# One SBUF residue for all moving tiles of a token group, and sixteen residues in turn

## The chip, the cores and the metric

The kernel runs on one core of one Trainium2 chip. The metric is the device time of one execution in microseconds (us), measured on the core. Three executions of the kernel before took 3115.2, 3115.26 and 3116.17 us; the median is 3115.26 us. Each engine runs its own instruction stream: PE multiplies matrices, and its weight loads (PEld) are shown apart from its matmuls; DVE and ACT do elementwise work, POOL as well; SP issues most of the DMAs.

## The reference

A long convolution is followed by a two-layer network. Cut to what matters:

```python
def _attn_ref(x, v, pos_emb, w1, w2):            # x, v: 4 x 12480 x 128
    h = np.maximum(pos_emb @ w1, 0.0) @ w2 * np.exp(-0.01 * pos)[:, None]
    y = np.fft.irfft(np.fft.rfft(x * v, n=2 * S, axis=1) * np.fft.rfft(h, n=2 * S, axis=0)[None], n=2 * S, axis=1)[:, :S]
    return x * y

def _moe_ref(x, w_in, w_out):                    # x: 49920 x 128; w_in: 128 x 2048; w_out: 2048 x 128
    h = np.maximum(x @ w_in, 0.0)
    return h * h @ w_out
```

## The kernel before

The convolution is a transform written as matmuls in four stages (s1 to s4), for the filter and for each of the four batches. The second part, the two-layer network, takes the 49,952 columns of s4's output in 98 token groups: two of 446 columns, then 512 or 510 columns each. The inner dimension of 2048 goes in eight blocks f of 256 columns. The network's stream of work is written out in one loop over groups and blocks; the transform stages of the next batch are generators from which the loop takes a step at three places (adv). The last groups, after all transform work, are called the tail here; the profile shows it from about 2670 us on.

Every float32 operand of the network is split in a high and a low part in a rounded float32 format, and one product is three matmuls (mm3, lines 92 to 97): high weights by high data (L95), low weights by high data (L96), high weights by low data (L97). For each group and block there are twelve of them: six that multiply w_in by the group's tokens (moving tiles zh and zl, into the PSUM tile A), and six that multiply w_out by the squared activations of an earlier block (moving tiles gh and gl, into O, or into F in the tail). The weights are the stationary operand, and each of these matmuls loads its own 128 by 128 weights first; the loads of the next matmul run beside the current one. In all there are 98 x 8 x 12 = 9408 such matmuls of the 13,442 that the program has.

Between them ACT makes r = relu(A) (L799) and squares (L802, L806), and DVE makes the rest (L804, L813) and gl = square - gh (L818). m_g and m_l do this; zsplit makes zh and zl of the next group (L781, L782) after zload has fetched it (zi).

Where the tiles lie. All are float32, two buffers each. The address of a tile within a partition is counted in bytes, and its residue here is that address modulo 512. As the program was built, the weight tiles wt start at 196,576 and follow each other 2048 bytes apart, with slices 512 bytes apart, so every weight slice of the network has residue 480. The tiles zh, zl, gh, gl and r of pool mp are 2048 or 4096 bytes long and stacked below the weights, so they have residue 480 too: zh at 159,712 and 161,760, gh at 176,096 and 180,192, gl at 184,288 and 188,384. In the tail a second pool, tp, on the other side of SBUF holds r, gh and gl of the odd blocks (line 882, `tail[0] if tail and f % 2 else mp`), and there gh and gl have residue 128 (gh at 131,712 and 135,808). In s4 the moving tiles ah and al have residue 128 or 448, and their weights, the four slices of a tile tb 448 bytes apart, many residues.

Of the kernel before, what the change touches and what calls it, by code (L numbers as in the profile page):

```python
# [7 lines left out]
F32 = mybir.dt.float32  # L8
F32R = mybir.dt.float32r
# [7 lines left out]
D = 128  # L17
# [9 lines left out]
GT = NT // NG  # L27
NS = NF // 2
GM = 512
NM = 2 + (B * NT - 2 * GT + GM - 1) // GM  # L30
GE = (B * NT - 2 * GT) // (NM - 2) // 2 * 2
GN = [GT, GT] + [GE + 2 * (k < (B * NT - 2 * GT - GE * (NM - 2)) // 2) for k in range(NM - 2)]
# [6 lines left out]
TH = 4  # L39
CW = 256  # L40
NCW = DFF // CW


@with_exitstack
def hyena_moe_kernel(
# [34 lines left out]
    def pool(name, side="left", **kw):  # L80
        return tc.tile_pool(name=name, bufs=kw.pop("bufs", 2), side=side, reuse_waits="tile", **kw)
# [17 lines left out]
    def load_weights(wp):  # L99
        raws = []  # L100
        for c in range(2 * NCW):
            raw = wp.tile([128, CW, 2], I32, tag="w", name="raw", bufs=2 * NCW)
            src = (w_in if c < NCW else w_out).bitcast(I32)[:, c % NCW * 2 * CW : (c % NCW + 1) * 2 * CW]
            nc.sync.dma_start(out=raw.rearrange("p a b -> p (a b)"), in_=src)
# [3 lines left out]
    def convert_weights(p, wp, raws, wt, chunks):  # L108
        V = nc.vector
        for c in chunks:  # L110
            low, high = raws[c][:, :, 0], raws[c][:, :, 1]
            mag, top, sgn = (p.tile([128, CW], I32, tag=k, name="cv") for k in ("cm", "ct", "cs"))
            mf = mag.bitcast(F32)
            tf = top.bitcast(F32)
            V.tensor_scalar(out=top, in0=high, scalar1=0x7FFFFFFF, scalar2=None, op0=ALU.bitwise_and)
            yield
            V.tensor_scalar(out=mf, in0=tf, scalar1=2.0**-15, scalar2=122880.0, op0=ALU.max, op1=ALU.min)
            yield
            V.tensor_scalar(out=top, in0=mag, scalar1=3, scalar2=0x7FFFFFFF, op0=ALU.logical_shift_left, op1=ALU.bitwise_and)
            yield  # L120
            V.tensor_scalar(out=mag, in0=low, scalar1=1, scalar2=None, op0=ALU.logical_shift_right)
            nc.gpsimd.tensor_copy(mf, mag)
            yield
            V.tensor_scalar(out=sgn, in0=high, scalar1=-0x80000000, scalar2=0x40000000, op0=ALU.bitwise_and, op1=ALU.bitwise_xor)
            yield
            V.tensor_tensor(out=top, in0=top, in1=sgn, op=ALU.bitwise_xor)
            wt[c] = wp.tile([128, 2, CW], F32R, tag="w", name="wt", bufs=2 * NCW)
            hi12, lo12 = wt[c][:, 0, :], wt[c][:, 1, :]
            nc.gpsimd.tensor_copy(hi12, tf)
            yield  # L130
            V.tensor_scalar(out=sgn, in0=top, scalar1=-0x800000, scalar2=None, op0=ALU.bitwise_and)
            yield
            V.scalar_tensor_tensor(out=mf, in0=mf, scalar=2.0**-51, in1=sgn.bitcast(F32), op0=ALU.mult, op1=ALU.mult)
            yield
            V.tensor_sub(out=tf, in0=tf, in1=hi12.bitcast(F32))
            yield
            V.tensor_add(out=lo12, in0=tf, in1=mf)
            yield
# [546 lines left out]
    def run(gen):  # L685
        for _ in gen:
            pass
# [6 lines left out]
    def take(name, *args, **kw):  # L694
        held[name] = ExitStack()
        return held[name].enter_context(pool(name, *args, **kw))
# [47 lines left out]
    cvp = take("cvp")  # L744
    conv = [convert_weights(cvp, wp, raws, wt, range(k, 2 * NCW, 2)) for k in range(2)]
    run(stage2(True, True, "left", during_s2f))
# [5 lines left out]
    held["tbb"].close()  # L752

    mp = ctx.enter_context(pool("mp", "right"))
    head = [mp.tile([D, GM], F32R, tag=k, name=k)[:, :GT] for k in ("zh", "zl")]
    s4 = stage4(0, done, take("t1p"))
    run(stage3(True, ft[0], lambda t: t == -12 and step(s4)))
    idle(12)
# [1 line left out]
    def wi(k, h, f):  # L760
        return wt[k * NCW + f // 2][:, h, f % 2 * 128 : (f % 2 + 1) * 128]

# [11 lines left out]
            at += n  # L774
        return zi

    def zsplit(zi):
        n = zi.shape[1]
        hi = mp.tile([D, GM], F32R, tag="zh", name="zh")[:, :n]
        lo = mp.tile([D, GM], F32R, tag="zl", name="zl")[:, :n]  # L780
        nc.scalar.copy(hi, zi)  # L781
        nc.gpsimd.tensor_sub(out=lo, in0=zi, in1=hi.bitcast(F32))  # L782
        return hi, lo

    def m_h(zT, f):
        A = psa.tile([128, 2, 512], F32, tag="A", name="A")
        for t in range(2):
            mm3(A[:, t, : zT[0].shape[1]], (wi(0, 0, 2 * f + t), wi(0, 1, 2 * f + t)), zT)
        return A

    def m_g(A, p, n, between, way):

        r = p.tile([128, 2, GM], F32, tag="r", name="r")[:, :, :n]
        hi = p.tile([128, 2, GM], F32R, tag="gh", name="gh")[:, :, :n]
        h = A[:, :, :n]
        nc.scalar.activation(r, h, AF.Relu)  # L799
        between()  # L800
        if way != "b":
            nc.scalar.activation(hi, r, AF.Square)  # L802
        if way == "p":
            nc.vector.scalar_tensor_tensor(out=h, in0=h, scalar=0.0, in1=r, op0=ALU.max, op1=ALU.mult)  # L804
            return p, h, hi, way
        nc.scalar.activation(r, r, AF.Square)  # L806
        return p, r, hi, way

    def m_l(st, share):
        p, g, hi, way = st  # L810
        lo = p.tile([128, 2, GM], F32R, tag="gl", name="gl")[:, :, : g.shape[2]]
        if way == "b":
            nc.vector.tensor_copy(hi, g)  # L813
        if share:
            nc.gpsimd.tensor_sub(out=lo[:, 1, :], in0=g[:, 1, :], in1=hi[:, 1, :].bitcast(F32))
            nc.vector.tensor_sub(out=lo[:, 0, :], in0=g[:, 0, :], in1=hi[:, 0, :].bitcast(F32))
        else:
            nc.vector.tensor_sub(out=lo, in0=g, in1=hi.bitcast(F32))  # L818
        return hi, lo
# [3 lines left out]
    def m_o(i, f, hl):  # L823
        if f == 0:
            O[0] = bank() if tail and not nxt[0] else pso.tile([128, 512], F32, tag="O", name="O")
        o = O[0][:, : GN[i]]
        for t in range(2):
            mm3(o, (wi(1, 0, 2 * f + t), wi(1, 1, 2 * f + t)), (hl[0][:, t, :], hl[1][:, t, :]), first=(f == 0 and t == 0), last=(f == NS - 1 and t == 1))
        if f == NS - 1:
            return i, o  # L830
        return None

    def m_out(last):
        if last is not None:
            i, o = last
            ot = mp.tile([D, GM], F32, tag="ot", name="ot", bufs=1)[:, : GN[i]]
            nc.scalar.copy(ot, o)
            nc.sync.dma_start(out=out[:, GO[i] : GO[i] + GN[i]], in_=ot)
# [11 lines left out]
    def adv(k):  # L850
        if k is None or nxt[0] == k:
            nxt[0] = next(stream, 0)

    def ready(i):
        b, at = divmod(GO[i] + GN[i] - 1, NT)
        while done[b] < 2 * (at // GT + 1):
            adv(None)

    def way(n):
        if not nxt[0]:  # L860
            return "b"
        if stage[0] == "s2":
            return "t" if n % 3 else "p"
        return "b" if stage[0] == "s3" else "p"

    late, pend, tail = [], [], []
# [4 lines left out]
    for i in range(NM):  # L871
        for f in range(NS):
            adv(1)
            A = m_h(zT, f)
            last = m_o(*pend.pop(0)) if len(pend) > 1 else None
            adv(2)
            if not nxt[0] and not tail:
                tail.append(ctx.enter_context(pool("tp")))
            late.append((i, f, m_g(A, tail[0] if tail and f % 2 else mp, GN[i], lambda: m_out(last), way(i * NS + f))))
            while len(late) > len(tail):  # L880
                x, y, st = late.pop(0)
                pend.append((x, y, m_l(st, False)))
            if i + 1 < NM:
                if f == (1 if i else 3):
                    ready(i + 1)
                    zi = zload(i + 1)
                if f == (4 if i else 6):
                    nzT = zsplit(zi)
            adv(3)
            n = i * NS + f  # L890
            if stage[0] != since[0]:
                since = stage[0], n + 4
            owed += EXTRA[done[1] > 0]
            if owed >= 1 and stage[0] in (("s3", "s4") if done[1] else ("s2", "s3", "s4")) and nxt[0] == 1 and n >= since[1]:
                owed -= 1
                since = stage[0], n + 3
                for k in range(1, 4):
                    adv(k)
        if i + 1 < NM:
            zT = nzT  # L900
    for x, y, st in late:
        pend.append((x, y, m_l(st, True)))
# [114 lines left out]
```

## Time and profile before

| what | value |
|---|---|
| median of three executions | 3115.26 us |
| span of the profiled execution, first to last instruction | 3112.0 us |
| what lies around the span, by the median | 3.3 us |
| PE busy | 3072.7 us, 99% of the span |
| PEld busy | 2579.8 us, 83% |
| DVE, ACT, POOL busy | 82%, 78%, 48% |
| granted TensorE clock, mean | 0.999 of full speed |

The time of the profiled execution itself is shown as its span alone, so the time of a run is taken as the span and 3.3 us. A matmul's row gives its whole passage through the engine, and matmuls overlap each other: one of 510 columns lasts about 390 ns, while the next starts about 228 ns after it. How fast the engine really goes is read from the starts in the timeline, or from a count of matmuls in a stretch of time.

### The profile page before, as it was taken

Reading aid. Unit: us, or ns where it says so; the run is one execution under the profiler, and the core shown is the slowest. Engines: PE = TensorE matmul, PEld = TensorE weight load, DVE = VectorE, ACT = ScalarE, POOL = GpSimd, SP = SyncE. Lnnn points to the kernel's source line nnn. Section 1 sums busy time; section 2 is a strip of 40 time slices with the busy share of each in tenths; the row PEclk is TensorE's granted clock in tenths of the full one; section 3 lists DMA queues with packets and bytes.
Section 4 is the critical chain, followed back from the end, with each engine's and each line's share of the span. In section 5 each row is a group of like instructions: output and inputs, shape, how many; then the busy total and the mean of one; then the engine's idle time right before and its main releaser. Section 6 shows DMA issues by size and latency. Waiting matters only on the chain.

```text
span 3112.0 us, 49107 instructions
## 1 busy us (share of the span) xinstructions
PE 3072.7 (99%) x16086; PEld 2579.8 (83%) x16086; DVE 2538.0 (82%) x3080; ACT 2419.1 (78%) x3130; POOL 1501.6 (48%) x1631
## 2 busy tenths in 40 slices
PE   9989999999999999999999999999999999999999
PEld 7767888888888888888888888888888888888887
DVE  7888898878877988878877898878877799777776
ACT  5556777777788777788888877787788887878787
POOL 1249765556544565546644575646644466000000
PEclk9999999999999999999999999999999999999999
DMA  5783574434200664434300375434410176100000
GB/s 184 263 294 99 137 166 137 124 111 145 67 21 15 151 161 132 130 91 127 115 15 21 80 176 144 133 92 121 124 51 14 36 168 156 33 24 24 24 26 20
DMA packets 342623, 323.11 MB, mean 104 GB/s; under 512 B 161968, under 2 KB 288800, under 8 KB 342368
## 3 DMA queue, kind: packets, MB, share of 16 engines
q1 hardware_dynamic: 313216, 272.25, 30.2%
q0 software_dynamic: 29152, 47.72, 6.4%
q8 instruction: 128, 2.10, 0.3%
q14 instruction: 127, 1.04, 0.1%
HBM read 231.78 MB, written 65.60 MB: 96 GB/s over the span
## 4 chain that ended last, share of the span: by engine, by line
PE 92%; POOL 2%; DMA 2%; DVE 2%; issue 1%; ACT 1%; SPq 0%; DVEq 0%; ACTq 0%; POOLq 0%
PE A L95 11%; PE A L97 11%; PE A L96 11%; PE O L97 9%; PE O L96 9%; PE O L95 9%; PE F L380 6%; PE F L492 6%; PE F L293 5%; PE F L97 4%; PE F L95 4%; PE F L96 4%; PE A L290 2%; PE A L291 1%; POOL W L405 1%
## 5 line engine op out<-in xcount | busy, mean ns | idle before, releaser
L799 ACT ACTIVATE r<-A 128x1024 f32<-128x1024 f32 (+2 forms) x784 | 803.8, 1025 | 420.8 <-PE A L97 407.0
L818 DVE TENSOR_TENSOR gl<-r,gh 128x1020 fp32r<-128x1020 f32 (+1 forms) x433 | 642.5, 1484 | 113.9 <-ACT r L806 80.0
L95 PE MATMUL A<-zh,wt 128*128 128x512 f32 (+2 forms) x1568 | 671.4, 428 | 0.9 <-DVE gl L818 0.9
L97 PE MATMUL A<-zl,wt 128*128 128x512 f32 (+2 forms) x1568 | 613.8, 391 | 0.0
L96 PE MATMUL A<-zh,wt 128*128 128x512 f32 (+2 forms) x1568 | 612.9, 391 | 0.0
L802 ACT ACTIVATE gh<-r 128x1024 fp32r<-128x1024 f32 (+2 forms) x461 | 486.9, 1056 | 62.8 <-PE O L96 57.2
L97 PE MATMUL O<-gl,wt 128*128 128x512 f32 (+2 forms) x1248 | 487.4, 391 | 4.2 <-DVE gl L818 4.2
L96 PE MATMUL O<-gh,wt 128*128 128x512 f32 (+2 forms) x1248 | 485.0, 389 | 0.0
L95 PE MATMUL O<-gh,wt 128*128 128x512 f32 (+2 forms) x1248 | 484.9, 389 | 0.0
L804 DVE SCALAR_TENSOR_TENSOR A<-A,r 128x1024 f32<-128x1024 f32 (+2 forms) x350 | 425.4, 1215 | 68.1 <-ACT r L799 66.5
L818 DVE TENSOR_TENSOR gl<-A,gh 128x1024 fp32r<-128x1024 f32 (+2 forms) x350 | 426.1, 1218 | 63.1 <-ACT gh L802 20.4
L806 ACT ACTIVATE r<-r 128x1020 f32<-128x1020 f32 (+1 forms) x434 | 460.3, 1061 | 12.5
L813 DVE CAST gh<-r 128x1020 fp32r<-128x1020 f32 (+1 forms) x323 | 225.6, 698 | 221.2 <-ACT r L806 152.7
L782 POOL TENSOR_TENSOR zl<-zi,zh 128x512 fp32r<-128x512 f32 (+2 forms) x97 | 126.4, 1303 | 522.4 <-ACT zh L781 506.1
L567 POOL TENSOR_TENSOR al<-W,ah 112x512 fp32r<-112x512 f32 x214 | 281.9, 1318 | 189.2 <-ACT ah L561 185.0
L501 POOL TENSOR_TENSOR W<-c 112x224 f32<-112x224 f32 x256 | 217.6, 861 | 285.7 <-ACT c L499 275.0
L97 PEld LDWEIGHTS A<-zl,wt 128*128 128x128 f32 x1568 | 294.6, 188 | 64.7
L95 PEld LDWEIGHTS A<-zh,wt 128*128 128x128 f32 x1568 | 295.5, 188 | 51.4 <-DVE gl L818 3.1
L96 PEld LDWEIGHTS A<-zh,wt 128*128 128x128 f32 x1568 | 296.2, 189 | 45.1
L417 POOL TENSOR_TENSOR W<-W,m 112x256 f32<-112x256 f32 x168 | 177.8, 1058 | 247.3 <-DVE m L415 233.1
L97 PEld LDWEIGHTS O<-gl,wt 128*128 128x128 f32 x1248 | 234.2, 188 | 54.5 <-DVE gl L818 5.9
L96 PEld LDWEIGHTS O<-gh,wt 128*128 128x128 f32 x1248 | 234.2, 188 | 50.6
(127 smaller groups left out, 5495.3 us busy)
## 6 DMA issues: line engine op xcount, KB each, us to landing
ht<-Hd SPq DMA_DIRECT2D x224, 256.0 KB
tb<-t POOLq DMA_DIRECT2D x224, 196.0 KB, 3.1
xt<-x SPq DMA_DIRECT2D x224, 112.0 KB
xt<-xs SPq DMA_DIRECT2D x96, 224.0 KB
vt<-vs SPq DMA_DIRECT2D x96, 224.0 KB
tb<-t2s SPq DMA_DIRECT2D x168, 112.0 KB
Hd<-he SPq DMA_DIRECT2D x28, 512.0 KB
zd<-zs SPq DMA_DIRECT2D x222, 64.0 KB
```

The source lines that it names most:

```text
L95: nc.tensor.matmul(o, lh, rh, start=first, stop=False)
L96: nc.tensor.matmul(o, ll, rh, start=False, stop=False)
L97: nc.tensor.matmul(o, lh, rl, start=False, stop=last)
L380: nc.tensor.matmul(U[:I, k * 256 : (k + 1) * 256], tb[:KP, k, :], a[:, k], start=True, stop=True)
L501: nc.gpsimd.tensor_sub(out=dst[:, 1], in0=c[:, :, 0:3:2], in1=c[:, :, 3:0:-2])
L567: eng.tensor_sub(out=lo, in0=w, in1=hi.bitcast(F32))
L799: nc.scalar.activation(r, h, AF.Relu)
L802: nc.scalar.activation(hi, r, AF.Square)
L804: nc.vector.scalar_tensor_tensor(out=h, in0=h, scalar=0.0, in1=r, op0=ALU.max, op1=ALU.mult)
L806: nc.scalar.activation(r, r, AF.Square)
L813: nc.vector.tensor_copy(hi, g)
L818: nc.vector.tensor_sub(out=lo, in0=g, in1=hi.bitcast(F32))
```

## The change

A helper `word` takes the place of the plain tile calls for zh, zl, gh and gl (SP = 128 floats, 512 bytes, more per tile): group i uses the tile from byte 32 * (i % 16) on. So all moving tiles of a group lie at one residue, 480 for group 0, 0 for group 1, 32 for group 2, and so on; after sixteen groups the row begins again, so the 98 groups go through it six times and two groups more. A tile of 88 floats in pool tp puts gh and gl of the tail's odd blocks at the same residue as those of its even blocks. The weights stay at residue 480, and r stays where its pool puts it, at residue 480 in mp.

```diff
+SP = 128
+TP = 88
...
-    head = [mp.tile([D, GM], F32R, tag=k, name=k)[:, :GT] for k in ("zh", "zl")]
+
+    def word(p, tag, i, n, t=None):
+        s = 8 * (i % 16)
+        w = p.tile([128, (t or 1) * GM + SP], F32R, tag=tag, name=tag)[:, s : s + (t or 1) * GM]
+        return w[:, :n] if t is None else w.rearrange("p (t n) -> p t n", t=t)[:, :, :n]
+
+    head = [word(mp, k, 0, GT) for k in ("zh", "zl")]
...
-    def zsplit(zi):
-        n = zi.shape[1]
-        hi = mp.tile([D, GM], F32R, tag="zh", name="zh")[:, :n]
-        lo = mp.tile([D, GM], F32R, tag="zl", name="zl")[:, :n]
+    def zsplit(i, zi):
+        hi, lo = (word(mp, k, i, GN[i]) for k in ("zh", "zl"))
...
-        hi = p.tile([128, 2, GM], F32R, tag="gh", name="gh")[:, :, :n]
+        hi = word(p, "gh", i, n, 2)
...
-        lo = p.tile([128, 2, GM], F32R, tag="gl", name="gl")[:, :, : g.shape[2]]
+        lo = word(p, "gl", i, GN[i], 2)
...
                 tail.append(ctx.enter_context(pool("tp")))
+                tail[0].tile([128, TP], F32, tag="tp", name="tp", bufs=1)
```

On every engine the instructions are the same, of the same shapes and in the same order. What differs in the built program is the start addresses of the four tiles (and those of r, which moves by whole multiples of 512 bytes in mp), and five instructions that wait for other semaphores, since the pools are some kilobytes larger and come to lie on other tiles that were there before: three on ACT at the start of the network, one more at the start of the tail that takes over its successor's wait, and the first L818 of the tail that writes in tp, on DVE, which now also waits for stores of s4 (L628).

## Rows read from the trace of the kernel before

**Rows 1.** The page, busy time: us, share of the span, instructions.
```profile
PE 3072.7 (99%) x16086; PEld 2579.8 (83%) x16086; DVE 2538.0 (82%) x3080; ACT 2419.1 (78%) x3130; POOL 1501.6 (48%) x1631
```
**Rows 2.** The page, chain that ended last, by engine.
```profile
PE 92%; POOL 2%; DMA 2%; DVE 2%; issue 1%; ACT 1%; SPq 0%; DVEq 0%; ACTq 0%; POOLq 0%
```
**Rows 3.** PE groups, shapes apart: count, busy us, mean ns, idle before.
```profile
L95 PE MATMUL A<-zh,wt 128*128 128x512 f32 x800 | 351.3, 439 | 0.8 <-DVE gl L818 0.8
L97 PE MATMUL A<-zl,wt 128*128 128x512 f32 x800 | 315.5, 394 | 0.0
L96 PE MATMUL A<-zh,wt 128*128 128x512 f32 x800 | 313.9, 392 | 0.0
L97 PE MATMUL O<-gl,wt 128*128 128x512 f32 x800 | 313.4, 392 | 4.2 <-DVE gl L818 4.2
L96 PE MATMUL O<-gh,wt 128*128 128x512 f32 x800 | 311.9, 390 | 0.0
L95 PE MATMUL O<-gh,wt 128*128 128x512 f32 x800 | 311.7, 390 | 0.0
...
L96 PE MATMUL A<-zh,wt 128*128 128x510 f32 x736 | 287.4, 390 | 0.0
L97 PE MATMUL A<-zl,wt 128*128 128x510 f32 x736 | 286.7, 390 | 0.0
...
L97 PE MATMUL O<-gl,wt 128*128 128x510 f32 x416 | 162.3, 390 | 0.0
L96 PE MATMUL O<-gh,wt 128*128 128x510 f32 x416 | 161.5, 388 | 0.0
L95 PE MATMUL O<-gh,wt 128*128 128x510 f32 x416 | 161.5, 388 | 0.0
...
L96 PE MATMUL F<-gh,wt 128*128 128x510 f32 x320 | 125.5, 392 | 0.0
L97 PE MATMUL F<-gl,wt 128*128 128x510 f32 x320 | 125.4, 392 | 0.0
...
L95 PE MATMUL F<-gh,wt 128*128 128x510 f32 x320 | 125.1, 391 | 0.0
```
**Rows 4.** PE timeline in the tail: start us, duration us, instruction.
```profile
3013.23 0.39 PE L95 MATMUL F<-gh,wt 128*128 128x510 f32 x1
...
3014.59 0.39 PE L95 MATMUL A<-zh,wt 128*128 128x510 f32 x1
...
3015.95 0.40 PE L95 MATMUL F<-gh,wt 128*128 128x510 f32 x1
...
3017.35 0.39 PE L95 MATMUL A<-zh,wt 128*128 128x510 f32 x1
```
**Rows 5.** Source L96: duration ns min/median/max, first and last start.
```profile
L96 PE MATMUL F<-ah,tb x448: 276/279/285, 329.3 to 2647.8; 112*112 112x256 f32 x150
...
L96 PE MATMUL F<-gh,wt x320: 387/395/397, 2672.9 to 3106.2; 128*128 128x510 f32 x160
```
**Rows 6.** Source L95 and L97, the same columns.
```profile
L95 PE MATMUL F<-ah,tb x448: 274/281/374, 329.1 to 2647.7; 112*112 112x256 f32 x150
...
L97 PE MATMUL F<-gl,wt x320: 387/394/398, 2673.1 to 3106.4; 128*128 128x510 f32 x160
```
**Rows 7.** PE timeline before the tail, the network's chain after a transform step.
```profile
995.97 0.48 PE L95 MATMUL A<-zh,wt 128*128 128x512 f32 x1
996.28 0.39 PE L96 MATMUL A<-zh,wt 128*128 128x512 f32 x1
...
997.44 0.39 PE L95 MATMUL O<-gh,wt 128*128 128x512 f32 x1
```
**Rows 8.** The page, costliest groups: DVE's and ACT's idle time, what ended it.
```profile
L799 ACT ACTIVATE r<-A 128x1024 f32<-128x1024 f32 (+2 forms) x784 | 803.8, 1025 | 420.8 <-PE A L97 407.0
L818 DVE TENSOR_TENSOR gl<-r,gh 128x1020 fp32r<-128x1020 f32 (+1 forms) x433 | 642.5, 1484 | 113.9 <-ACT r L806 80.0
```
**Rows 9.** Source L628, the stores of s4: duration, first and last start.
```profile
L628 SPq DMA_DIRECT2D zd<-zs x444: 407/556/1869, 339.1 to 2653.3; - x148
```

More of the change, by code (lines that the diff above doesn't have):

```diff
@@ L789, in m_h, with m_g @@
         return A
-    def m_g(A, p, n, between, way):
+    def m_g(A, p, i, between, way):
+        n = GN[i]
         r = p.tile([128, 2, GM], F32, tag="r", name="r")[:, :, :n]
-        hi = p.tile([128, 2, GM], F32R, tag="gh", name="gh")[:, :, :n]
+        hi = word(p, "gh", i, n, 2)
         h = A[:, :, :n]
@@ L804, in m_g @@
             nc.vector.scalar_tensor_tensor(out=h, in0=h, scalar=0.0, in1=r, op0=ALU.max, op1=ALU.mult)
-            return p, h, hi, way
+            return p, i, h, hi, way
         nc.scalar.activation(r, r, AF.Square)
-        return p, r, hi, way
+        return p, i, r, hi, way
     def m_l(st, share):
-        p, g, hi, way = st
-        lo = p.tile([128, 2, GM], F32R, tag="gl", name="gl")[:, :, : g.shape[2]]
+        p, i, g, hi, way = st
+        lo = word(p, "gl", i, GN[i], 2)
         if way == "b":
@@ L878, in hyena_moe_kernel @@
                 tail.append(ctx.enter_context(pool("tp")))
-            late.append((i, f, m_g(A, tail[0] if tail and f % 2 else mp, GN[i], lambda: m_out(last), way(i * NS + f))))
+                tail[0].tile([128, TP], F32, tag="tp", name="tp", bufs=1)
+            late.append((i, f, m_g(A, tail[0] if tail and f % 2 else mp, i, lambda: m_out(last), way(i * NS + f))))
             while len(late) > len(tail):
@@ L887, in hyena_moe_kernel @@
                 if f == (4 if i else 6):
-                    nzT = zsplit(zi)
+                    nzT = zsplit(i + 1, zi)
             adv(3)
```

## The prediction

> **What bounds the kernel now.** I read the busy times first: PE is busy for 99% of the span, the next engine for 83 or 82% [rows 1]. The chain that ended last is PE for 92% of the way [rows 2]. So the time is that of PE's stream of matmuls, and I ask what one matmul of the network costs. The PE groups with shapes apart show it as a duration [rows 3]: 388 to 394 ns, apart from L95 A<-zh, of which many come right after a transform's matmuls and contain the restart (the first takes 0.31 us to the next start, later ones 1.16/5 = 0.23 [rows 7]). Idle time before these groups is about 5 us in all, so PE waits for nobody, and what it does is given by its own pace. ACT idles 421 us before L799, nearly all behind PE, and DVE 114 us before L818 [rows 8].
>
> The pace is not one number. In the tail, where no transform work lies between, four blocks of six matmuls each follow each other [rows 4]. The first two read gh in pool mp and zh, both at residue 480, that of the weights: 3014.59 - 3013.23 = 1.36 us and 3015.95 - 3014.59 = 1.36 us, 226.7 ns for each matmul. The next six read gh and gl of an odd block, which lie in tp at residue 128: 3017.35 - 3015.95 = 1.40 us, 233.3 ns each. Shape, weights' residue, clock and engine are the same; what differs is where the moving tile lies. The durations say it too: the F<-gh and F<-gl matmuls range only from 387 to 398 ns [rows 5, 6], and a duration 1 ns longer goes with a start 1 ns later (0.39 beside 226.7, 0.40 beside 233.3). So the trace holds the operation of the change at two residues of sixteen.
>
> **The change part by part.** It adds and removes no instruction and reorders none. It shifts where 9408 matmuls read their moving operand, and where ACT, DVE and POOL write it.
>
> The matmuls. Mean duration now, from the 13 groups of rows 3 other than the first: their busy times add up to 3001.8 us for 7680 matmuls, 390.9 ns. That is above 388, the locked pace of residue 480 (which 226.7 ns stands for), for two reasons: the tail's odd blocks at residue 128, and the 512-column groups, which run at 390 to 394 though all at residue 480. Afterwards one sixteenth of the groups is at residue 480 as now, and fifteen sixteenths are at others, of which the trace knows one. From below: all others as good as the fastest of rows 5 and 6, 387 ns, -3.9 ns x 9408 x 15/16 = -34 us. From above: all as slow as the slowest, 398 ns, +7.1 ns x 8820 = +63 us. Between these ends I take the middle, 392.5 ns, since the two known places lie near either end (388 for residue 480, about 395 for 128, by the medians of rows 5 and 6, where both kinds are mixed): +1.6 ns x 8820 = +14 us.
>
> A second look at places comes from s4, whose moving tiles have two residues while the weights' slices have many: there the same matmul of 256 columns lasts from 274 or 276 to 285 ns, with medians of 281 and 279 [rows 5, 6]. So places better than the middle by 5 to 7 ns and worse by 4 to 6 both exist, which keeps both ends open and gives no reason to leave the middle.
>
> The Trainium skill speaks against any effect: TensorE: Matmul & The Clock Gate, in Step-by-step: what each phase is for, says that PE has two independent SBUF read ports, one for the moving data and one for weight loads, so that loading the next tile's weights takes no read bandwidth from the running matmul. By that rule the place beside the weights could not matter and the sum would be 3115 us; the 1.36 and 1.40 us of rows 4 do not agree with it.
>
> The writers. gl's subtraction reads r and gh, which lay at one residue and will not. The trace has no such pair in mp. At nothing I bound it from below; from above, if each of the 433 L818 on r took 100 ns more, a sixteenth of its 1484 ns, that is 43 us of DVE, beside 114 us of idle time before them [rows 8]: hidden. I take nothing. If that cover were gone, PE would wait at L97 O<-gl, where it waits 4.2 us now [rows 3].
>
> The waits. The first L818 in tp now waits for s4's stores too. The last of these is issued at 2653.3 us [rows 9], the tail's first F<-gh starts at 2672.9 [rows 5]: landed long before. The ACT waits stand once, at the start; they can cost a microsecond or two or nothing. I take nothing.
>
> Sum: span 3112.0 + 14 + 3.3 around it = 3129.8, against the median of 3115.26: 3130 us.
>
> **The rivals.**
> - *The shared residue is a bad place* and the sweep visits mostly better ones (faster). One mechanism: reading moving data and weights at equal offsets collides most, other offsets less. For it: the 512-column groups at 392 and 394 ns though at residue 480 [rows 3], and s4's fast matmuls, 7 ns below their median [rows 6]. Against it: the one other place seen in the network is 7 ns slower. It decides once the fifteen other residues average below 390.9 ns. With 388 ns, -2.9 x 8820 = -26 us: 3089 us.
> - *All other residues are as 128* (much slower): 480 is the one good place, because it is the weights' own. For it: rows 4. Against it: s4, which has no single good place. At 395.5 ns, +4.6 x 8820 = +41 us: 3156 us.
> - *The residue does nothing on average*: it is the pool's place in SBUF that makes tp slow, or the sweep's mean falls where the kernel is now. For it: 390.9 ns is already almost in the middle of 387 and 398. That gives 3115 us, within 6 us. The rule of two ports in the Trainium skill (TensorE: Matmul & The Clock Gate) would bring the same time.
>
> **How the numbers follow.** The forecast, a mean of the other residues at 391.6 to 394 ns (3122 to 3143 us), has a chance of 0.40; much slower 0.18; no effect 0.17; faster 0.25. A change under 0.2%, 6 us, can't be told from none in this kernel. So slower 0.58, same 0.17, faster 0.25. The likeliest case's own range is 3122 to 3143 us. The range that holds 8 in 10 reaches up to just past the second rival and down to most of the first: 3095 to 3158 us.
>
> **What the profile after would show.** Every group of 96 matmuls runs at its own pace, and the pace comes back sixteen groups later; the medians of L96 F<-gh in the tail spread evenly instead of lying at two values; the mean of rows 3 rises to 392 to 393 ns; idle time before PE's groups stays under 10 us. Groups at residue 480 keep 226.7 ns in the tail. It would be wrong if groups of all residues had one duration (the third rival), if the groups at 480 were among the slowest (the first), or if PE's idle time behind gl or r grew by tens of us, which would mean that the writers pay and not the reader.

## The result and the profile after

Three executions of the changed kernel took 3136.6, 3138.47 and 3140.43 us, median 3138.47, against 3115.26 before: 1.0075 of the time, 95% interval 1.0056 to 1.0095. That is 23.2 us more; 3130 was forecast, with a range of 3095 to 3158.

The line numbers of the network are shifted by two to seven: L97, L98, L99 now are the three matmuls that were L95, L96, L97, and L825 is the subtraction that was L818. The page of the kernel after, its span and busy times:

```profile
span 3134.8 us, 49110 instructions
...
PE 3096.8 (99%) x16086; PEld 2581.9 (82%) x16086; DVE 2538.9 (81%) x3080; ACT 2416.4 (77%) x3130; POOL 1505.3 (48%) x1631
```

Against [rows 1] PE is busy for 24.1 us more, and the span is 22.8 us longer. No other engine has more than 4 us of new work: the time is in PE's matmuls alone. The PE groups of the kernel after, shapes apart (count, busy us, mean ns, idle before):

```profile
L97 PE MATMUL A<-zh,wt 128*128 128x512 f32 x800 | 353.3, 442 | 0.6 <-DVE gl L825 0.6
L97 PE MATMUL O<-gh,wt 128*128 128x512 f32 x800 | 316.1, 395 | 0.0
L99 PE MATMUL O<-gl,wt 128*128 128x512 f32 x800 | 316.1, 395 | 3.6 <-DVE gl L825 3.6
L99 PE MATMUL A<-zl,wt 128*128 128x512 f32 x800 | 315.6, 395 | 0.0
L98 PE MATMUL A<-zh,wt 128*128 128x512 f32 x800 | 315.2, 394 | 0.0
L98 PE MATMUL O<-gh,wt 128*128 128x512 f32 x800 | 315.0, 394 | 0.0
...
L99 PE MATMUL A<-zl,wt 128*128 128x510 f32 x736 | 289.2, 393 | 0.0
L98 PE MATMUL A<-zh,wt 128*128 128x510 f32 x736 | 289.1, 393 | 0.0
L98 PE MATMUL O<-gh,wt 128*128 128x510 f32 x416 | 163.4, 393 | 0.0
L97 PE MATMUL O<-gh,wt 128*128 128x510 f32 x416 | 163.3, 393 | 0.0
L99 PE MATMUL O<-gl,wt 128*128 128x510 f32 x416 | 163.3, 393 | 0.0
...
L97 PE MATMUL F<-gh,wt 128*128 128x510 f32 x320 | 125.6, 393 | 0.0
L99 PE MATMUL F<-gl,wt 128*128 128x510 f32 x320 | 125.5, 392 | 0.0
L98 PE MATMUL F<-gh,wt 128*128 128x510 f32 x320 | 125.4, 392 | 0.0
```

They answer to [rows 3]. Each kind is 0 to 5 ns longer. The 13 groups that the sum used (without the first) now have 3022.8 us for the same 7680 matmuls, 393.6 ns against 390.9: 2.7 ns x 9408 is 25 us, the whole difference. Idle time before them has not grown. The writers have not paid: on the page of the kernel after, the subtraction takes 1483 ns where it took 1484 [rows 8], and ACT waits behind PE a little more:

```profile
L806 ACT ACTIVATE r<-A 128x1024 f32<-128x1024 f32 (+2 forms) x784 | 802.7, 1024 | 433.1 <-PE A L99 421.3
L825 DVE TENSOR_TENSOR gl<-r,gh 128x1020 fp32r<-128x1020 f32 (+1 forms) x433 | 642.2, 1483 | 115.9 <-ACT r L813 80.5
```

How the pace goes from residue to residue shows in the tail, where each group is 96 matmuls back to back. The matmuls on gh and gl come about three blocks after those on zh and zl, so the first 42 of a group's 96 are mixed with matmuls that read tiles of the group before, at its residue. Each stretch below is therefore the second half alone: a group's last 48 matmuls, up to the next group's first zh matmul, for residues 480, 0, 32, 64, 96, 128, 160, 192 and 224 in turn (kernel after; the stretch, its length in us, PE busy us and the count of matmuls that touch it, granted clock, DMA):

```profile
2738.28:2749.16 10.88, 10.88 (x50) 1.00 0.10 25
2760.14:2771.02 10.88, 10.88 (x49) 1.00 0.09 21
2782.11:2793.15 11.04, 11.04 (x49) 1.00 0.09 21
2804.31:2815.51 11.20, 11.20 (x49) 1.00 0.10 26
2826.62:2837.71 11.09, 11.09 (x49) 1.00 0.09 22
2848.90:2860.10 11.20, 11.20 (x49) 1.00 0.09 23
2871.21:2882.09 10.88, 10.88 (x50) 1.00 0.07 17
2893.14:2904.34 11.20, 11.20 (x50) 1.00 0.10 25
2915.39:2926.28 10.89, 10.89 (x50) 1.00 0.09 23
```

The length divided by 48 is the distance of two starts: 226.7 ns at residues 480, 0 and 160, 230.0 at 32, 231.0 at 96, and 233.3 at 64, 128 and 192. The ninth stretch repeats the first, and the seven groups after it repeat the second to the eighth (10.88, 11.04, 11.20, 11.09, 11.20, 10.88 and 11.20 us): the pace comes back after eight groups, 256 bytes, and not after sixteen. So there are eight places, three good and five worse, and the worst three are as slow as the blocks at residue 128 in [rows 4].

Which places are good hangs on the columns too. The PE group L98 on gh in three stretches of the kernel after, one group each: at residue 480 with 512 columns (1323.3 to 1354.4 us), at residue 0 with 512 (1354.6 to 1382.8) and at residue 0 with 510 (2308.2 to 2339.9):

```profile
L98 PE MATMUL O<-gh,wt 128*128 128x512 f32 x16 | 6.2, 390 | 0.0
```
```profile
L98 PE MATMUL O<-gh,wt 128*128 128x512 f32 x16 | 6.3, 394 | 0.0
```
```profile
L98 PE MATMUL O<-gh,wt 128*128 128x510 f32 x16 | 6.2, 389 | 0.0
```

For half of the groups, those with 512 columns, residue 0 is one of the bad places. Over the whole trace, the L98 matmuls on gh with 512 columns have 391 ns on average at residues 480 and 224, 392 at 32 and 288, and 393 to 396 at the other twelve.

### The profile page after: what moved, and what is told of

Read it like the earlier page. It is cut to its first block, busy times and chain, and to the rows that moved or that the text cites. A ratio compares the mean times of both kernels' runs of the same rounds, so it can differ in the third digit from the quotient of the medians.

```text
span 3134.8 us, 49110 instructions
## 1 busy us (share of the span) xinstructions
PE 3096.8 (99%) x16086; PEld 2581.9 (82%) x16086; DVE 2538.9 (81%) x3080; ACT 2416.4 (77%) x3130; POOL 1505.3 (48%) x1631
## 4 chain that ended last, share of the span: by engine, by line
PE 92%; DMA 2%; DVE 2%; POOL 2%; issue 1%; ACT 1%; SPq 1%; DVEq 0%; ACTq 0%; POOLq 0%
PE A L97 11%; PE A L99 11%; PE A L98 11%; PE O L99 9%; PE O L97 9%; PE O L98 9%; PE F L382 6%; PE F L494 5%; PE F L295 5%; PE F L97 4%; PE F L99 4%; PE F L98 4%; PE A L292 2%; PE A L293 1%; DMA ht<-Hd 1%
## 5 line engine op out<-in xcount | busy, mean ns | idle before, releaser
L825 DVE TENSOR_TENSOR gl<-r,gh 128x1020 fp32r<-128x1020 f32 (+1 forms) x433 | 642.2, 1483 | 115.9 <-ACT r L813 80.5
L97 PE MATMUL A<-zh,wt 128*128 128x512 f32 (+2 forms) x1568 | 674.7, 430 | 1.0 <-DVE gl L825 0.9
L99 PE MATMUL A<-zl,wt 128*128 128x512 f32 (+2 forms) x1568 | 616.5, 393 | 0.0
L98 PE MATMUL A<-zh,wt 128*128 128x512 f32 (+2 forms) x1568 | 616.0, 393 | 0.0
L99 PE MATMUL O<-gl,wt 128*128 128x512 f32 (+2 forms) x1248 | 491.1, 393 | 3.6 <-DVE gl L825 3.6
L97 PE MATMUL O<-gh,wt 128*128 128x512 f32 (+2 forms) x1248 | 491.2, 394 | 0.0
L98 PE MATMUL O<-gh,wt 128*128 128x512 f32 (+2 forms) x1248 | 490.0, 393 | 0.0
L825 DVE TENSOR_TENSOR gl<-A,gh 128x1024 fp32r<-128x1024 f32 (+2 forms) x350 | 426.1, 1217 | 64.5 <-ACT gh L809 21.8
L99 PEld LDWEIGHTS A<-zl,wt 128*128 128x128 f32 x1568 | 294.9, 188 | 67.4
L97 PEld LDWEIGHTS A<-zh,wt 128*128 128x128 f32 x1568 | 295.4, 188 | 52.1 <-DVE gl L825 2.7
L98 PEld LDWEIGHTS A<-zh,wt 128*128 128x128 f32 x1568 | 296.7, 189 | 46.6
L99 PEld LDWEIGHTS O<-gl,wt 128*128 128x128 f32 x1248 | 234.6, 188 | 60.2 <-DVE gl L825 6.1
L98 PEld LDWEIGHTS O<-gh,wt 128*128 128x128 f32 x1248 | 234.6, 188 | 54.0
```

The lines of the kernel that those rows point to most:

```text
L97: nc.tensor.matmul(o, lh, rh, start=first, stop=False)
L98: nc.tensor.matmul(o, ll, rh, start=False, stop=False)
L99: nc.tensor.matmul(o, lh, rl, start=False, stop=last)
```

## The experiments

For each kernel the tail's pace is read from one row: the stretch 2700 to 3090 us, all of it the network's matmuls, and how many of them PE did in 390 us. The view counts every matmul that touches the stretch, one or two more than start in it, so the quotient lies 0.2 to 0.3 ns below the distance of two starts. In the kernel before and after (stretch, length, PE busy and count, then PEld, DVE, ACT and POOL likewise, granted clock, DMA):

```profile
2700.00:3090.00 390.00, 390.00 (x1706) 320.04 (x1705) 286.30 (x284) 311.42 (x320) 23.28 (x18) 1.00 0.08 24
```
```profile
2700.00:3090.00 390.00, 390.00 (x1692) 317.74 (x1690) 284.00 (x283) 308.05 (x317) 22.05 (x17) 1.00 0.08 24
```

390 us over the count is 228.6 ns before and 230.5 after. The theory was that the difference of two residues, that of the moving tile less that of the weights, sets the pace; the rivals, each with its run, were the larger pools and waits, the moving residue alone, and the going on from one residue to the next.

**All at 480.** The diff against the kernel after:

```diff
-        s = 8 * (i % 16)
+        s = 0
```

> The pools and waits of the changed kernel, but every group at offset 0, so all moving tiles at residue 480 like the weights, in the tail too. Theory (the place of the moving tile against the weights sets the pace): the 23 us are gone, and the tail's odd blocks, which took 1.40 us for six matmuls in the kernel before, take 1.36: 3115 less about 3 us, 3112 us. Rival (larger pools, other waits or the writers cost the time): it stays near 3138 us.

Measured: 3107.71 us beside 3111.77 for the kernel before on the same chip, 0.9985 (0.9976 to 0.9994). The tail of this run, the same view:

```profile
2700.00:3090.00 390.00, 390.00 (x1722) 322.42 (x1721) 288.81 (x287) 315.26 (x324) 23.35 (x18) 1.00 0.08 24
```

226.5 ns for a matmul on average (226.7 by the starts). Pools, waits and the shapes of the accesses are those of the kernel after. All of the loss is gone, and 4 us beyond it: the odd blocks of the tail, at 128 before, now have the pace of the even ones. So it was the residues, and the added waits cost nothing that shows.

**All at 64, weights at 480.** `s = 24` in the same place.

> As the first run, but every group at residue 64, with the weights at 480. In the changed kernel's tail the groups at residue 64 start a matmul every 233 to 235 ns, those at 480 every 227 to 228. Theory: about 5.2 ns x 9408 matmuls above the kernel before, 3164 us. Rival (only the going on from residue to residue costs): 3115 us.

Measured: 3147.87 us, 1.0113 (1.0099 to 1.0127), 36 us above the kernel before where 49 were expected. In the tail, the same view and the group of L97 on zh:

```profile
2700.00:3090.00 390.00, 390.00 (x1673) 313.76 (x1672) 281.61 (x280) 306.20 (x315) 23.17 (x18) 1.00 0.08 24
```
```profile
L97 PE MATMUL A<-zh,wt 128*128 128x510 f32 x278 | 110.5, 397 | 0.0
```

233.1 ns, as the groups at 64 had in the sweep. The loss in the tail is as expected: 1706/1673 is 2.0% more of some 440 us, 9 us. The other 27 us, over some 7500 matmuls before the tail, are 3.6 ns each and not 5.2: among the transform's steps a bad place costs less. The rival would have had 3115 us; one fixed bad residue is enough.

**All at 64, weights at 64.** The weights move with a tile ahead of theirs, and everything below with them:

```diff
-SP = 128
-TP = 88
+SP = 0
+TP = 112
...
+    ctx.enter_context(pool("sp", "right")).tile([128, 104], F32, tag="sp", name="sp", bufs=1)
     wp = ctx.enter_context(pool("wp", "right"))
...
-        s = 8 * (i % 16)
+        s = 0
```

> Moving tiles at residue 64 and the weights moved to residue 64 too, all tiles of the network lying 416 bytes lower. Theory (the difference of the two residues counts): 3112 us, as with both at 480. Rival (the moving tile's own residue counts): 3164 us, as with moving tiles at 64 and weights at 480.

Measured: 3105.36 us, 0.9973 (0.9962 to 0.9985). In the tail:

```profile
2700.00:3090.00 390.00, 390.00 (x1723) 322.38 (x1722) 288.25 (x287) 314.77 (x323) 21.95 (x17) 1.00 0.08 24
```

226.4 ns with the moving tiles where they were in the run before, which had 233.1. What changed between the two is the weights' residue: 42.5 us. So the moving tile's own residue doesn't set the pace. This is the lowest median of the study.

**Weights of the two layers apart.** All moving tiles at 384, w_in at 384, w_out at 480 (besides the lines below, `SP = 0`, `TP = 64` and `s = 0`):

```diff
+            if c == NCW:
+                wp.tile([128, 24], F32, tag="ws", name="ws", bufs=1)
-            raw = wp.tile([128, CW, 2], I32, tag="w", name="raw", bufs=2 * NCW)
+            raw = wp.tile([128, CW, 2], I32, tag=f"w{c // NCW}", name="raw", bufs=NCW)
...
-            wt[c] = wp.tile([128, 2, CW], F32R, tag="w", name="wt", bufs=2 * NCW)
+            wt[c] = wp.tile([128, 2, CW], F32R, tag=f"w{c // NCW}", name="wt", bufs=NCW)
```

> All moving tiles at one residue, 384; w_in's weights at 384 as well, w_out's at 480. Theory (difference of residues): zh and zl keep 227 to 230 ns from start to start, gh and gl slow to 233, since their difference is 160 modulo 256, at which the changed kernel's tail groups (residues 128 and 384) run at 233: about 5 ns x 4704, 3137 us. In the tail the sixth zl matmul, beside which w_out's first weights are loaded, should be slow if the next load is what collides, and the sixth gl matmul fast; the other way round if a matmul's own weights count. Rival (own residue of the moving tile): all four tiles at one pace.

Measured: 3130.89 us, 1.0061 (1.0047 to 1.0075), 19 us above the kernel before where 24 were expected. The PE groups of the stretch 2700 to 3090 us:

```profile
L98 PE MATMUL F<-gh,wt 128*128 128x510 f32 x282 | 111.8, 396 | 0.0
L97 PE MATMUL F<-gh,wt 128*128 128x510 f32 x282 | 111.7, 396 | 0.0
L99 PE MATMUL F<-gl,wt 128*128 128x510 f32 x282 | 111.1, 394 | 0.0
L99 PE MATMUL A<-zl,wt 128*128 128x510 f32 x283 | 110.4, 390 | 0.0
L97 PE MATMUL A<-zh,wt 128*128 128x510 f32 x283 | 110.0, 389 | 0.0
L98 PE MATMUL A<-zh,wt 128*128 128x510 f32 x283 | 109.9, 388 | 0.0
```

The six matmuls of w_in keep 388 to 390, those of w_out have 394 to 396, with all moving tiles at one residue: again the difference. Whose weights count was to be read at the seams, and they gave no clear answer. By the starts in the trace, the tail's sixth zl matmul takes 229.6 ns on average (226.7 the four before it) and the sixth gl matmul 229.2 (232.1 the one before): both half way. Neither "the next load" nor "its own weights" was right by itself.

**Half the columns of the low weights**, all moving tiles at 64, weights at 480:

```diff
-        nc.tensor.matmul(o, ll, rh, start=False, stop=False)
+        if ll.shape[0] == 128:
+            o2, ll = o[:64], ll[:, :64]
+        else:
+            o2 = o
+        nc.tensor.matmul(o2, ll, rh, start=False, stop=False)
...
-        s = 8 * (i % 16)
+        s = 24
```

> Moving tiles at residue 64, weights at 480, as in the second run, but the matmul with the low weights (the second of three) takes only 64 of its 128 weight columns, for the network and the filter's first layer; the low part of the other 64 outputs is left out. Its stream stays 510 or 512 columns long, only its weight load is shorter, and that load runs beside the first matmul of the three. Theory (the load of the next weights collides with the moving read of the running matmul): the first matmul's distance to the next start falls from 235 to some 225 ns, the other two keep 230 to 235; about 3136 matmuls x 9 ns below the second run, near 3120 us. Rival (a place costs the moving read by itself): all three keep their distance, 3148 us.

Measured, in one execution: 3139.0 us. In the tail, the group of L97 on zh and the same view as before:

```profile
L97 PE MATMUL A<-zh,wt 128*128 128x510 f32 x280 | 110.4, 394 | 0.0
```
```profile
2700.00:3090.00 390.00, 390.00 (x1681) 286.11 (x1680) 281.69 (x281) 306.68 (x314) 22.01 (x17) 1.00 0.08 24
```

The expectation failed. L97, beside which the halved load runs, has 394 ns where all columns gave 397; 10 ns were expected. About 9 us went, not 28. The count in the tail shows how much came back: PE did 1722 matmuls in 390 us with everything at 480, 1673 at 64 with whole loads and 1681 here, so 8 of the 49 lost ones returned, a sixth. A sixth of the loaded columns is also what the edit took away, half of them in one matmul of three. The gain isn't all at the matmul beside the shorter load: by the starts in the trace, the three distances are 236.0, 234.0 and 230.0 ns with whole loads and 232.5, 231.6 and 232.5 here.

**The same with everything at 480**, `s = 0`:

> As the run with 64 of the low weights' 128 columns, the same part of the low weights left out, but all moving tiles at residue 480, like the weights. In the run with all columns and everything at 480 a matmul of the tail started every 226.7 ns, all three kinds alike; 510 columns alone need 212.5 ns at 2.4 GHz. If the 14 ns between are collisions with the load beside the stream, the first of the three, beside which the halved load runs, falls to about 220 ns: 3136 x 7 ns, 3086 to 3090 us. If 226.7 ns is a floor that the load's length doesn't set, nothing changes: 3108 us.

Measured: 3113.8 us, 0.9998 (0.9989 to 1.0007). In the tail:

```profile
2700.00:3090.00 390.00, 390.00 (x1722) 291.75 (x1721) 289.38 (x287) 314.43 (x323) 23.23 (x18) 1.00 0.08 24
```

PEld is busy for 291.75 us and not 322.42, and PE does the same 1722 matmuls. The 220 ns that the halved load was to bring did not come: with everything at 480, 226.5 ns is a floor that the length of this load does not set. What sets it is open; no run here has matmuls of the network without loads beside them. The 3113.8 us stand beside 3113.66 for the kernel before in the same series; by the ratios this run is 0.0013 above the one with all columns, and the two intervals overlap.

**Steps of 16 bytes through 256**, weights at 64 as in the third run: `SP = 64`, `TP = 112`, `s = 4 * (i % 16)`.

> Weights at residue 64 as in the third run; the groups go on by 16 bytes through 256, so that differences of 0, 16, ... 240 bytes are seen, the odd multiples of 16 for the first time. Theory: the pace depends on the difference modulo 256; the even ones repeat the changed kernel's tail (227 to 228 ns at 0, 32 and 192, 230 to 231 at 64 and 128, 233 at 96, 160 and 224) and the odd ones lie between their neighbours; total near 3130 us. Rival (the pace goes with the absolute residue): the even ones come out in another order than by difference.

Measured, in one execution: 3133.66 us. The second halves of the tail's groups, at differences 0, 16, 32, 64, 96, 128, 192 and 240 (same view as the stretches above):

```profile
2734.95:2745.83 10.88, 10.88 (x50) 1.00 0.09 26
2756.82:2768.02 11.20, 11.20 (x49) 1.00 0.09 23
2778.99:2789.87 10.88, 10.88 (x49) 1.00 0.08 22
...
2823.27:2834.31 11.04, 11.04 (x49) 1.00 0.09 23
...
2867.43:2878.63 11.20, 11.20 (x50) 1.00 0.09 23
...
2912.29:2923.49 11.20, 11.20 (x50) 1.00 0.09 24
...
3000.94:3011.82 10.88, 10.88 (x49) 1.00 0.10 25
...
3067.48:3078.36 10.88, 10.88 (x49) 1.00 0.09 25
```

Here residue 64 is a good place and in the kernel after it was one of the worst; by difference the two agree: 226.7, 226.7, 230.0, 233.3 and 226.7 ns at differences 0, 32, 64, 96 and 192 in both, and the same holds at 160 and 224 (233.1 and 233.3 here). The weights lie at 64 throughout and the pace still changes, so the weights' own residue does not set it either. Difference 128 is the exception, 233.3 here and 231.0 there; the difference modulo 256 is not the whole account, and what else counts at 128 is open. The odd multiples were expected between their neighbours; 16 and 48 have 233.3 and 233.1, above both, and 240 has 226.7, below 224. Four differences, 0, 32, 192 and 240, share the best pace, and none is better.

**The low moving tiles alone at 64**, all else at 480: `s = 24 if tag in ("zl", "gl") else 0`.

> All at residue 480 but zl and gl, the low moving tiles, which lie at 64. Theory (a matmul's pace goes by the difference of its own moving tile to the weights): the third of the three matmuls slows from 226.7 to some 233 ns, the first two keep 226.7 to 228: 3136 x 6 ns, about 19 us above the run with all at 480, 3127 us. Rival (the pace of a whole chain is set by its worst place): all three slow, 3148 us.

Measured: 3135.28 us beside 3113.66, 1.0061 (1.0044 to 1.0077), 21.6 us above the kernel before; with the 0.9985 of the run with all at 480 that is 0.76%, 24 us above that run, where 19 were expected. The tail's PE groups and count:

```profile
L97 PE MATMUL A<-zh,wt 128*128 128x510 f32 x282 | 111.7, 396 | 0.0
...
L98 PE MATMUL A<-zh,wt 128*128 128x510 f32 x282 | 110.8, 393 | 0.0
...
L99 PE MATMUL A<-zl,wt 128*128 128x510 f32 x282 | 110.4, 392 | 0.0
```
```profile
2700.00:3090.00 390.00, 390.00 (x1689) 318.11 (x1688) 282.11 (x281) 308.32 (x317) 22.06 (x17) 1.00 0.08 24
```

The sum was near and the place of the loss was not: the two high matmuls, whose tiles lie well, have 396 and 393 ns, and the one at the bad place 392, all three above the 388 of the run with all at 480. That all three slow is what the rival said, but not its size: 33 matmuls of 1722 are lost in the 390 us and not 49, two thirds of the loss for a third of the tiles. So a bad place is paid by its neighbours in the chain as well, as far as the recorded starts and ends tell which matmul waits.

**Shorter groups**, both residues at 64, `NM = 3 + ...` for one group more, 504 or 506 columns each:

> Both residues at 64 as in the third run, but 97 groups of 504 or 506 columns instead of 96 of 510 or 512 behind the first two. The 512-column groups there need 226.8 to 230.4 ns a matmul, 510 ones 226.5 to 228.3. If a matmul's time goes with its columns (2.4 GHz, 0.42 ns a column) a matmul starts every 224 to 225 ns and only the fixed part of 96 more matmuls is added: some 3 us less than the third run, 3102 us. If the pace locks at the same 226.7 ns, it is 96 x 227 ns = 22 us more, 3127 us.

Measured: 3125.17 us, 1.0040 (1.0026 to 1.0054). In the tail:

```profile
2700.00:3090.00 390.00, 390.00 (x1722) 323.23 (x1721) 286.32 (x288) 312.45 (x323) 22.98 (x18) 1.00 0.08 24
```

226.5 ns again, with four to six columns fewer: over these few columns the pace is locked, and the shorter groups only added matmuls. By the ratios that cost 21 us over the third run, where 22 were expected. It is not locked for every width. The first two groups of all these kernels have 446 columns, and in the third run's trace five of their matmuls take 1.00 us:

```profile
345.61 0.36 PE L97 MATMUL O<-gh,wt 128*128 128x446 f32 x1
...
346.61 0.37 PE L99 MATMUL O<-gl,wt 128*128 128x446 f32 x1
```

That is 200 ns each, 27 less than for 504 to 510 columns. Between 446 and 504 columns no run was made.

## Why the prediction was right, point by point

- *What bounds the kernel.* Right: PE was busy 24.1 us longer and the span grew by 22.8, with nothing gained or lost on other engines.
- *The two places of rows 4 are the operation of the change.* Right, and now shown: going to one place and moving the weights after it brings 42.5 us back.
- *The mean of the fifteen other residues, the one large term.* Its mechanism was right and its size was off. It was put at 392.5 ns, the middle of the shortest and longest F<-gh duration. With the sixteenth at residue 480 left at 390.9, the measured mean of 393.6 makes the others 393.8: +2.9 ns x 8820 = 25 us, not 14. The shapes show where the middle failed. The 510-column groups of the sum now average 392.6 ns (1444.8 us for 3680 matmuls), the middle itself, and the 512-column groups 394.5 (1578.0 us for 4000). The middle was read from 510-column matmuls of the tail and put on both shapes, although rows 3 had the 512-column groups at 390 to 394 with all at 480; they have fewer good places. That the middle fits 510 columns was a guess that came true: the eight places of the tail lie at both ends and average 230.1 ns, where the middle of 226.7 and 233.3 is 230.0.
- *The sum.* 3112.0 + 14 + 3.3 makes 3129.3 and not 3129.8, a slip that the forecast of 3130 hardly feels.
- *s4 as a second look.* It promised places 5 to 7 ns better than the middle; its own two rows, each against its own median, have 7 and 3. In the network no group of 504 or more columns in any run's tail had a pace under 226.6 ns from start to start, 3.4 below the middle. Its matmuls have half the columns and 112 weights, and its spread said nothing of these.
- *Writers and waits at nothing.* Right: 1483 against 1484 ns, and the run with all at 480 has the same waits at 3107.71 us.
- *The rivals.* The faster one fell: the shared residue is not a bad place but one of three good ones. What spoke for it, 392 to 394 ns in the 512-column groups, is the pace of 512 columns among transform steps, with all at 480. Much slower fell as well: in the tail residues 0, 160, 224 and 256 have 480's pace. No effect on average fell by the interval. The two read ports of the Trainium skill (TensorE: Matmul & The Clock Gate, Step-by-step: what each phase is for) would have brought it; they do not agree with the 42.5 us that moving the weights made.
- *What the profile after would show.* The pace came back after eight groups, not sixteen; the groups at residue 480 kept 226.7 ns in the tail, in their second halves; the mean rose to 393.6, a little over the 392 to 393 named; idle time stayed under 10 us. The places are not spread evenly: three lie at either end.

Open: how the weight loads and the moving reads hinder each other. That they do is shown, since moving either one changes the pace; that a load collides with the read that runs beside it is argued only. The halved loads took a sixth of the columns and a sixth of the loss, which would fit a loss in proportion to the loaded columns; one run alone says so, and the low tiles alone, a third of the streams and two thirds of the loss, do not fit a loss that each stream makes for itself. The seams point both ways, and how a stall is passed on in a chain was not settled. Open as well is whether both residues at 64 (0.9962 to 0.9985) are better than both at 480 (0.9976 to 0.9994): the intervals overlap.

## What to carry to other kernels

Where back-to-back matmuls of this kind bound a kernel (rounded float32, 128 by 128 weights loaded for each, some 500 columns), lay moving tiles and weights at equal byte addresses modulo 256, and check tiles that a second pool adds: 1.4% lay between the best and the worst kernel here, and no wait shows it, only the matmuls' durations and their count in a stretch. When a pace is known at two places of many, the middle of the seen ends is a fair guess with a wide range, and only for the shape that it was read from; here the other shape made the error. A duration that varies by place is worth reading in the quietest stretch of the program, where one group follows another without waits.

## What the runs showed of the hardware that was not expected

- The pace of a chain is locked over a few columns: 504 or 506 columns and 510 columns alike give 1722 matmuls in 390 us, 226.5 ns each, and loading half the columns of a third of the weights leaves it there. With 446 columns it is 200 ns.
- The place repeats after 256 bytes. By the difference between moving tile and weights, 16 bytes on one side of the equal address cost 6.7 ns (233.3 against 226.7), and 16 bytes on the other side nothing.
- One badly placed tile of three slows its well-placed neighbours: 396 and 393 ns for them, 392 for itself, 388 where all lie well.
